# Four places in a PSUM bank for the output sum of a decode block, folded into two fresh banks near the end

## The chip, the cores and the metric

The kernel runs on one core of a Trainium2 chip. The metric is the device time of one execution in microseconds (us). Before the change, three runs gave 210.86, 211.17 and 211.27 us, median 211.17.

## What is computed

One decode step for 4 sequences of one token, model width 576. The normalised input feeds an attention block and an MLP block, and their outputs are added to the input:

```
xn = layernorm(A_x)
out = A_x + A(xn) + B(xn)

A: q = xn @ wq                      # 32 query heads of 128, 16 key/value heads
   k, v = the last 2048 of 8192 positions of k_cache, v_cache
   o = softmax(q k^T / sqrt(128)) v
   return o.reshape(4, 1, 4096) @ wo

B: (one position: its four shifts of h read only padding, so hs is 0)
   return xn + gelu(layernorm(xn) @ w3) @ w4     # w3: 576x4608, w4: 4608x576
```

All operands are bfloat16. The two products that end in the output, with `wo` (4096 rows) and with `w4` (4608 rows), and the sum xn + A_x are added up in PSUM, the matmul's accumulation memory, in one output sum of 4 x 576.

## The kernel before

The keys and values (16 heads, in 8 pairs, 4 MB each for K and for V) are read by indirect DMAs from the POOL queue (`load_kv`, L125) into three buffers. `flush_loads` issues the next load of a list written out by hand whenever a buffer comes free. The last items of the list are `wo`'s fourth quarter (L147) and `w4` (`load_w4`, L163). w4 has 36 rows of 128 x 576 (a "row" here is one 128-deep slice of its 4608 rows). It is loaded in six pieces, rows 0-17, 18-24, 25-29, 30-33, 34 and 35, each with a semaphore of its own, so a matmul waits only for its piece.

The schedule is manual: each engine carries out its instructions in the order of the program text. Each round t of the main loop transposes a pair's keys on DVE (L281), computes scores on PE (L395), and finishes the softmax, the product with V (L459) and the output projection of earlier pairs. Since two pairs' heads (four heads, or eight with the repeat) make one quarter of `wo`, every second round ends in `o_turn` (transpose), `o_sum`, `o_spread` (8 matmuls into R, L489), `o_pick` (two DVE operations on R, L499 and L502, that leave the operand `op`) and `o_proj` (L241).

The output sum is a PSUM tile of 128 partitions x 288 columns, cleared to 0 by L222. Its first 288 output columns stand in partitions 0 to 3, the other 288 in partitions 32 to 35. `acc_matmuls` (L238 to L242) adds a list of terms to it: each term is one 4-column weight and one 576-column row, split into two matmuls of 288 columns, one for each half. A matmul whose output starts at partition 0, 32, 64 or 96 uses the part of the PE array that belongs to that place. `o_proj` gives 8 terms, 16 matmuls; the w4 rows (`mlp_out`) give 36 terms, 72 matmuls.

In the last round (pair 7), `acc_split` (L229 to L235) moves the second half into a bank of its own: ACT copies 4 x 288 to SBUF (L232), and a float32 matmul with the identity writes it into a buffer of the pool of score tiles (tag S, three buffers; L234). A float32 matmul is carried out as two passes. After that, the two halves can be read by two engines at once. The end of the program is, from line 681: `o_scale`, `o_turn`, `o_sum`, `o_spread`, `o_pick`, `o_proj` for the last quarter, then w4's rows in order, then DVE copies the first half to `fin` (L694) and ACT the second (L696), and SP stores it (L697).

Of the kernel before, what the change touches and what calls it, by code (L numbers as in the profile page):

```python
# [8 lines left out]
ACT = mybir.ActivationFunctionType  # L9
ALU = mybir.AluOpType  # L10
AX = mybir.AxisListType
BF16 = mybir.dt.bfloat16
F32 = mybir.dt.float32
# [9 lines left out]
def kernel(  # L23
# [14 lines left out]
    nc = tc.nc  # L38
    P = 128
    B, Sq, D = A_x.shape  # L40
# [8 lines left out]
    NF = F // P  # L49
# [3 lines left out]
    QD = 32  # L53
# [6 lines left out]
    NI = 2  # L60
    CW = D // NI
    NW = SC * QD
# [20 lines left out]
    const = ctx.enter_context(tc.tile_pool(name="const", bufs=1))  # L83
    small = ctx.enter_context(tc.tile_pool(name="small", bufs=2))
    ps_s = ctx.enter_context(tc.tile_pool(name="ps_s", bufs=3, space=PSUM))
# [43 lines left out]
    first = wop.tile([P, WOR * D], BF16, tag="wo", name="first")  # L129
# [26 lines left out]
    W4_PIECES = [0, NFH, NF - 11, NF - 6, NF - 2, NF - 1, NF]  # L156
# [42 lines left out]
    ident_f = ident_w[:, 0:P]  # L199
# [18 lines left out]
    gT = const.tile([P, NF, B], BF16, name="gT")  # L218
    op = const.tile([P, WOR, B], BF16, name="op")

    acc = ps_acc.tile([P, CW], F32, name="acc")
    nc.vector.memset(acc[:], 0.0)  # L222

    accs = [acc, acc]

    def acc_of(i):
        return accs[i][i * QD:i * QD + B, 0:CW]

    def acc_split():  # L229
        rows = slice(QD, QD + B)  # L230
        half = const.tile([P, CW], F32, name="half")
        nc.scalar.activation(out=half[rows], in_=acc_of(1), func=ACT.Copy)  # L232
        accs[1] = ps_s.tile([P, NW], F32, tag="S", name="acc1")
        nc.tensor.matmul(out=acc_of(1), lhsT=ident_f[rows, rows], rhs=half[rows],  # L234
                         start=True, stop=False, skip_group_check=True)  # L235


    def acc_matmuls(terms):  # L238
        for lhsT, rhs in terms:
            for i in range(NI):  # L240
                nc.tensor.matmul(out=acc_of(i), lhsT=lhsT, rhs=rhs[:, i * CW:(i + 1) * CW],  # L241
                                 start=False, stop=False, skip_group_check=True)  # L242

    def layernorm(dst_f, dst_bf, src):
        st = small.tile([B, 2, nc.vector.BN_STATS_DIM], F32, tag="ln_st")
        nc.vector.bn_stats(out=st[:, 0, :], in_=src[:, 0:D // 2])
        nc.vector.bn_stats(out=st[:, 1, :], in_=src[:, D // 2:D])
        mv = small.tile([B, nc.vector.BN_AGGR_DIM], F32, tag="ln_mv")
        nc.vector.bn_aggr(out=mv[:], in_=st[:].rearrange("p a s -> p (a s)"))
        rstd = small.tile([B, 1], F32, tag="ln_rstd")  # L250
        nc.vector.tensor_scalar_add(out=rstd[:], in0=mv[:, 1:2], scalar1=eps)
        nc.gpsimd.tensor_tensor(out=rstd[:], in0=rstd[:], in1=neg_half[:], op=ALU.pow)  # L252
        nc.vector.tensor_scalar(out=dst_bf[:], in0=src[:], scalar1=mv[:, 0:1], scalar2=rstd[:, 0:1],
                                op0=ALU.subtract, op1=ALU.mult)
        if dst_f is not None:
            nc.vector.tensor_scalar(out=dst_f[:], in0=src[:], scalar1=mv[:, 0:1], scalar2=rstd[:, 0:1],
                                    op0=ALU.subtract, op1=ALU.mult)
# [20 lines left out]
    def k_transpose(t, q):  # L278
        src = kv_tiles["K", t][:].bitcast(I32)[:, q * QC:(q + 1) * QC, :].rearrange("p c (ib i) -> p ib c i", i=QD)
        kt = ktp.tile([P, 2, QC, QD], I32, tag="kt")  # L280
        nc.vector.transpose(out=kt[:], in_=src)  # L281
        kts[t, q] = kt
# [3 lines left out]
    for kb in range(NQD):  # L286
        nc.gpsimd.tensor_copy(out=sel[:, :, :, kb, :],
                              in_=ident_bf[:].rearrange("p (ib i e) -> p ib e i", ib=2, e=2))
# [23 lines left out]
    for g in range(2):  # L312
        nc.gpsimd.tensor_copy(out=same_j[:, g * 2 * QD:(g + 1) * 2 * QD].rearrange("p (e s j) -> p e s j", e=2, j=NJ),
                              in_=sel_j[:].unsqueeze(2).to_broadcast([P, 2, NSL, NJ]))
# [10 lines left out]
    xsum = xn_f  # L325
    nc.gpsimd.tensor_tensor(out=xsum[:], in0=xn_f[:], in1=x_bf[:], op=ALU.add)
    acc_matmuls([(ident_f[0:B, 0:B], xsum)])
    ln2_bf = part(D, B)
    layernorm(None, ln2_bf, xn_bf)
# [26 lines left out]
    for r in range(2):  # L356
        nc.vector.tensor_copy(out=q_bf[:, r],
                              in_=qT_ps[:, r].rearrange("p u (g x) -> p g u x", g=NQD)[:, :, :, 0:B])
    qs_ps = ps_m.tile([P, Hkv, 4, rep, B], F32, tag="m", name="qs_ps")
    for ie in range(4):  # L360
        ib, e = divmod(ie, 2)
        nc.tensor.matmul(out=qs_ps[:, :, ie], lhsT=sel[:, ib, e].rearrange("p k i -> p (k i)"),
                         rhs=q_bf.rearrange("p r g u b -> p (r g u b)"), start=True, stop=True)
    for kb in range(NQD):
        rows = slice(kb * QD, (kb + 1) * QD)
        dst = qz[rows, ZP:].rearrange("p (t i m) -> p t i m", i=4, m=P)[:, :, :, kb * QD:kb * QD + NJ]
# [20 lines left out]
    def k_scores(t, q, sl):  # L387
        u, s = q // 2, q % 2 * 2 + sl
        kt = kts[t, q][:].bitcast(BF16)
        if sl:  # L390
            kts.pop((t, q))
        for ie in range(4):
            ib, e = divmod(ie, 2)
            z0 = (t * 4 + ie) * P + ZP - s * NJ
            nc.tensor.matmul(out=S_ps[t, u][:], lhsT=qz[:, z0:z0 + P],  # L395
                             rhs=kt[:, ib, sl * SC:(sl + 1) * SC, e:2 * QD:2].rearrange("p c k -> p (c k)"),
                             start=False, stop=False, skip_group_check=True)
# [75 lines left out]
    def o_sum(t):  # L473
        oT = st.pop(("oT", t))
        v = oT[:].rearrange("p s (g x) -> p (s g) x", g=2).rearrange("p g (e x) -> p e x g", e=2)[:, :, 0:NJ]
        k = 2 * t % WOQ
        if k == 0:
            st["on"] = small.tile([P, WOH, B], BF16, tag="on", name="on")
        with nc.allow_low_precision("summed in float32"):
            nc.vector.reduce_sum(out=st["on"][:, k * rep:(k + 2) * rep, :].rearrange("p (e r) b -> p e (r b)", e=2),  # L480
                                 in_=v, axis=AX.X)

    def o_spread(h):
        if h % WOQ < WOQ - 1:
            return
        on = st.pop("on")
        R = ps_m.tile([P, WOR, WOH, B], F32, tag="m", name="R")
        for i in range(WOR):
            nc.tensor.matmul(out=R[:, i].rearrange("p h b -> p (h b)"),  # L489
                             lhsT=sel_wo[:, i].rearrange("p h d -> p (h d)"),  # L490
                             rhs=on[:].rearrange("p h b -> p (h b)"), start=True, stop=True)
        st["R"] = R

    def o_pick(h):
        if h % WOQ < WOQ - 1:
            return
        R = st.pop("R")
        mk = small.tile([P, WOR, WOH, B], BF16, tag="mk")
        nc.vector.tensor_tensor(out=mk[:], in0=R[:],  # L499
                                in1=own[:].unsqueeze(1).unsqueeze(3).to_broadcast([P, WOR, WOH, B]), op=ALU.mult)  # L500
        with nc.allow_low_precision("one term is not zero"):
            nc.vector.reduce_sum(out=op[:], in_=mk[:].rearrange("p i h b -> p i b h"), axis=AX.X)  # L502

    def o_proj(h):
        if h % WOQ < WOQ - 1:
            return
        acc_matmuls([(op[:, i, :], wo_tiles[h // WOQ][:, i, :]) for i in range(WOR)])
# [41 lines left out]
        nc.gpsimd.tensor_scalar(out=u[:], in0=u[:], scalar1=0.5, scalar2=0.5, op0=ALU.mult, op1=ALU.add)  # L549
        nc.gpsimd.tensor_tensor(out=gT[:], in0=u[:], in1=xs[:], op=ALU.mult)  # L550

    def mlp_out(lo, hi):
        w4 = w_tiles["w4"]
        acc_matmuls([(gT[:, u, :], w4[:, u, :]) for u in range(lo, hi)])


    G_AT = 3
# [84 lines left out]
    k_scores(hl, 1, 0)  # L642
    o_turn(o)
    k_scores(hl, 1, 1)
    acc_split()
    k_transpose(hl, 3)
    free_one()
    o_sum(o)
# [33 lines left out]
    o_turn(hl)  # L682
    o_sum(hl)
    o_spread(2 * hl + 1)
    o_pick(2 * hl + 1)
    o_proj(2 * hl + 1)
    for lo, hi in zip(W4_PIECES, W4_PIECES[1:]):
        mlp_out(lo, hi)

    fin = const.tile([B, D], out.dtype)  # L690
    for i in range(NI):
        dst = fin[:, i * CW:(i + 1) * CW]
        if i == 0:
            nc.vector.tensor_copy(out=dst, in_=acc_of(i))  # L694
        else:
            nc.scalar.activation(out=dst, in_=acc_of(i), func=ACT.Copy)  # L696
    nc.sync.dma_start(out=o2, in_=fin[:])  # L697


# [28 lines left out]
```

## Time and profile before

| what | us |
|---|---|
| median of three runs | 211.17 |
| the profiled execution | 210.84 |
| its span, first to last instruction | 209.07 |
| PE, DVE, ACT, POOL busy in the span | 145.9, 124.8, 29.7, 31.4 |
| start of the last `o_proj` | 200.63 |
| start of w4's first row on PE | 201.61 |
| start of the copies to fin | 206.36 |
| bytes moved | 87.32 MB, 418 GB/s over the span |

In the profile, PE stands for matmuls and PEld for the loads of their weights; DVE is VectorE, ACT ScalarE, POOL GpSimd, SP SyncE. A line of a timeline has the start in us from the span's start, the time to the end of the group, the engine, the line of the program, the operation, the tiles (written <- read), the shape and the number of instructions. In square brackets stands how long the engine was idle before it and what ended that. The page divides the span into 40 slices; one digit is a tenth of a slice, and PEclk is the clock that TensorE was granted, in tenths of the full one. The profiled execution's time holds 1.77 us that lie outside the span.

### The profile page before, as it was taken

How to read it: one execution, taken by the hardware profiler on the slowest of the kernel's cores; microseconds unless marked ns; L12 is line 12 of the kernel's file. 1: busy time of each engine (PE TensorE's matmuls, PEld its weight loads, DVE VectorE, ACT ScalarE, POOL GpSimd, SP SyncE). 2: the span in 40 equal slices, each digit the busy share in tenths (PEclk: the TensorE clock that was granted, in tenths of full speed). 3: DMA queues.
4: the chain of work that ended last, by engine and by line, in shares of the span. 5: the costliest groups of instructions: out<-in, count | busy, mean ns of one | idle time of the engine just before them, and what ended most of it. 6: DMA issues, size and time to landing. Idle time of an engine off the chain costs nothing.

```text
span 209.1 us, 2179 instructions
## 1 busy us (share of the span) xinstructions
PE 145.9 (70%) x879; PEld 60.6 (29%) x892; DVE 124.8 (60%) x177; ACT 29.7 (14%) x61; POOL 31.4 (15%) x62
## 2 busy tenths in 40 slices
PE   0249199649669943059998794587967937996974
PEld 0013033222215310014443431143324311453552
DVE  5410779994189700097928990989089818986120
ACT  6402500110102011003001201020002010303100
POOL 5680001003200110000133011001010161100000
PEclk9999859996957995558999999597999985998899
DMA  7999999999999999999999999999999999999991
GB/s 302 401 464 439 401 445 442 439 401 445 458 397 437 447 422 414 397 456 464 414 404 478 414 408 419 474 426 408 464 433 411 447 439 414 451 439 397 423 402 71
DMA packets 4156, 87.32 MB, mean 418 GB/s; under 512 B 489, under 2 KB 497, under 8 KB 1201
## 3 DMA queue, kind: packets, MB, share of 16 engines
q0 software_dynamic: 3840, 82.45, 91.8%
q1 hardware_dynamic: 296, 4.72, 5.5%
q8 instruction: 7, 0.11, 0.2%
q14 instruction: 5, 0.03, 0.0%
q10 hardware_dynamic: 8, 0.00, 0.0%
HBM read 87.17 MB, written 0.00 MB: 417 GB/s over the span
## 4 chain that ended last, share of the span: by engine, by line
DMA 42%; PE 32%; DVE 13%; issue 8%; POOL 3%; ACT 0%; POOLq 0%; DVEq 0%; ACTq 0%
DMA kn<-in_A_k_cache_dram,row 32%; PE S L395 14%; PE O L459 10%; DMA vn<-in_A_v_cache_dram,row 9%; DVE kt L281 8%; PE acc L241 3%; PE g_ps L522 1%; DVE pt L440 1%; PE oT L470 1%; PE gT_ps L535 1%; DVE mx L401 1%; POOL kn L125 0%; PE R L489 0%; PE S L383 0%; POOL rstd L252 0%
## 5 line engine op out<-in xcount | busy, mean ns | idle before, releaser
L281 DVE STREAM_TRANSPOSE kt<-kn 128x2048 int32<-128x2048 int32 x32 | 73.7, 2306 | 46.2 <-DMA kn<-in_A_k_cache_dram,row 44.0
L395 PE MATMUL S<-kt,qz 128*128 128x512 bf16 x243 | 76.2, 438 | 33.7 <-DVE kt L281 32.0
L395 PEld LDWEIGHTS <-qz 128*128 128x128 bf16 x256 | 23.4, 103 | 71.1 <-issue 54.4
L459 PE MATMUL O<-vn,pt 128*64 128x512 bf16 x256 | 36.0, 413 | 5.5 <-DVE kt L281 2.4
L440 DVE STREAM_TRANSPOSE pt<-E 64x512 bf16<-64x512 bf16 x32 | 22.1, 690 | 1.2 <-ACT E L431 0.9
L431 ACT ACTIVATE E<-S,bias 128x512 bf16<-128x512 f32 x16 | 10.9, 683 | 75.1 <-DVE bias L424 75.1
L125 POOL DMA_INDIRECT vn<-in_A_v_cache_dram,row x8 | 7.7, 962 | 91.3 <-DVE kt L281 87.2
L459 PEld LDWEIGHTS <-pt 128*64 128x64 bf16 x256 | 13.7, 116 | 22.2 <-issue 13.7
L464 ACT ACTIVATE O_sb<-O,rd 128x512 f32<-128x512 f32 x8 | 5.5, 687 | 62.5 <-PE O L459 62.5
L125 POOL DMA_INDIRECT kn<-in_A_k_cache_dram,row x8 | 7.9, 990 | 42.5 <-PE O L459 23.3
L401 DVE TENSOR_REDUCE mx<-S 128x1 f32<-128x512 f32 x16 | 10.7, 667 | 0.1
L522 PE MATMUL g_ps<-w_sb,ln2T 128*32 128x512 bf16 (+1 forms) x50 | 5.2, 489 | 2.9 <-DMA w_sb<-in_B_w_dram 2.9
L383 PE MATMUL S<-negbig,ohT 4*128 4x512 bf16 x16 | 6.4, 398 | 0.2 <-ACT E L431 0.2
L241 PE MATMUL acc<-wo_sb,op 128*4 128x288 bf16 x64 | 4.6, 286 | 1.0 <-DVE op L502 1.0
L480 DVE TENSOR_REDUCE on<-oT 128x16 bf16<-128x128 f32 x8 | 2.3, 286 | 4.9 <-PE oT L470 4.7
L470 PE MATMUL oT<-ident_w,O_sb 128*128 128x128 f32 x32 | 5.2, 286 | 0.0
L339 PE MATMUL q_ps<-wq_sb,xnT 128*32 128x512 bf16 x40 | 4.5, 629 | 0.9 <-DMA wq_sb<-in_A_wq_dram 0.9
L470 PEld LDWEIGHTS oT<-ident_w,O_sb 128*128 128x128 f32 x32 | 4.1, 149 | 2.2 <-issue 0.9
L241 PE MATMUL acc<-w_sb,gT 128*4 128x288 bf16 x72 | 4.7, 286 | 0.0
L163 POOL DMA_DIRECT2D w_sb<-in_B_w_dram x6 | 3.3, 579 | 8.1 <-DMA vn<-in_A_v_cache_dram,row 8.1
L424 DVE TENSOR_SCALAR bias<-bp 128x1 f32<-128x1 f32 x8 | 1.3, 159 | 5.3 <-PE bp L419 5.3
L404 DVE TENSOR_SCALAR dm<-sel_g,mx 128x8 bf16<-128x8 bf16 x16 | 3.9, 243 | 0.6
(100 smaller groups left out, 79.2 us busy)
## 6 DMA issues: line engine op xcount, KB each, us to landing
wo_sb<-in_A_wo_dram POOLq DMA_DIRECT2D x4, 1152.0 KB, 23.5
w_sb<-in_B_w_dram POOLq DMA_DIRECT2D x1, 4608.0 KB, 29.4
wq_sb<-in_A_wq_dram SPq DMA_DIRECT2D x1, 4096.0 KB, 13.8
w_sb<-in_B_w_dram POOLq DMA_DIRECT2D x1, 2592.0 KB, 29.1
w_sb<-in_B_w_dram POOLq DMA_DIRECT2D x2, 576.0 KB, 31.6
w_sb<-in_B_w_dram POOLq DMA_DIRECT2D x1, 1008.0 KB, 31.0
w_sb<-in_B_w_dram POOLq DMA_DIRECT2D x1, 720.0 KB, 32.2
wq_sb<-in_A_wq_dram SPq DMA_DIRECT2D x1, 512.0 KB, 3.3
```

What stands on the lines that cost most here:

```text
L125: nc.gpsimd.indirect_dma_start(tl[:].rearrange("p c d -> p (c d)"), None, k_rows if kind == "K" else v_rows, bass.IndirectOffsetOnAxis(ap= ...
L241: nc.tensor.matmul(out=acc_of(i), lhsT=lhsT, rhs=rhs[:, i * CW:(i + 1) * CW], start=False, stop=False, skip_group_check=True)
L281: nc.vector.transpose(out=kt[:], in_=src)
L383: nc.tensor.matmul(out=S_ps[t, u][:].rearrange("p (c k) -> p c k", k=QD), lhsT=ohT[:], rhs=negbig[:].unsqueeze(1).to_broadcast([B, SC, QD] ...
L395: nc.tensor.matmul(out=S_ps[t, u][:], lhsT=qz[:, z0:z0 + P], rhs=kt[:, ib, sl * SC:(sl + 1) * SC, e:2 * QD:2].rearrange("p c k -> p (c k)" ...
L401: nc.vector.reduce_max(out=mx[:], in_=S_ps[t, u][:], axis=AX.X)
L431: nc.scalar.activation(out=E[t, u][:].rearrange("p c k -> p (c k)"), in_=S_ps.pop((t, u))[:], func=ACT.Exp, scale=scale, bias=st["bias", t ...
L440: nc.vector.transpose(out=pts[t % 2 * NU + u][rows, :, e * QD:(e + 1) * QD], in_=e_in[rows])
L459: nc.tensor.matmul(out=O_ps[t][rows], lhsT=pts[t % 2 * NU + u][:, c, :], rhs=vn[:, u, :, c, :], start=(u == 0 and c < 2), stop=False, skip ...
L464: nc.scalar.activation(out=O_sb[t][:], in_=O_ps.pop(t)[:], func=ACT.Copy, scale=st.pop(("rd", t))[:, 0:1])
L470: nc.tensor.transpose(out=oT[:, s, :], in_=o[:, s, :], identity=ident_w[:, s * NJ:s * NJ + P])
L522: nc.tensor.matmul(out=g_ps[g * QD:(g + 1) * QD], lhsT=ln2T[:, k, :], rhs=cols[:, :, i0:i0 + n], start=(j == 0), stop=False, skip_group_ch ...
```

## The change

The output sum gets four places in its bank: partitions 0, 32, 64 and 96. Terms with an even number in their list go to the first two places, those with an odd number to the other two. `acc_split` is gone. Near the end, ACT copies the whole sum (128 x 288) to SBUF (`half`), two fresh banks are opened in the pool of score tiles (one for each half of the columns), and w4's rows from 25 on go there. Between rows 29 and 30, two float32 matmuls with a matrix of zeros and ones, `fold`, add `half`'s places 0 and 2 to the first bank, and 1 and 3 to the second. `fold` is made by one POOL operation in the preamble, behind the two identity matrices. w4's rows 0 to 17 are moved ahead of the last `o_pick` and `o_proj`. Loads and their order are not changed.

```diff
-    accs = [acc, acc]
-
-    def acc_of(i):
-        return accs[i][i * QD:i * QD + B, 0:CW]
-
-    def acc_split():
-        rows = slice(QD, QD + B)
+    def acc_of(g):
+        return acc[g * QD:g * QD + B, :]
+
+    def acc_matmuls(terms):
+        for k, (lhsT, rhs) in enumerate(terms):
+            for i in range(NI):
+                nc.tensor.matmul(out=acc_of(k % 2 * NI + i), lhsT=lhsT, rhs=rhs[:, i * CW:(i + 1) * CW],
+                                 start=False, stop=False, skip_group_check=True)
+
+    fold = const.tile([P, NI * B], F32, name="fold")
+    nc.gpsimd.tensor_tensor(out=fold[:].rearrange("p (i b) -> p i b", i=NI),
+                            in0=ident_f[:, 0:2 * QD].rearrange("p (i x) -> p i x", i=NI)[:, :, 0:B],
+                            in1=ident_f[:, 2 * QD:P].rearrange("p (i x) -> p i x", i=NI)[:, :, 0:B], op=ALU.add)
+    sums = []
+
+    def sum_of(i):
+        return sums[i][i * QD:i * QD + B, 0:CW]
+
+    def sum_open():
         half = const.tile([P, CW], F32, name="half")
-        nc.scalar.activation(out=half[rows], in_=acc_of(1), func=ACT.Copy)
-        accs[1] = ps_s.tile([P, NW], F32, tag="S", name="acc1")
-        nc.tensor.matmul(out=acc_of(1), lhsT=ident_f[rows, rows], rhs=half[rows],
-                         start=True, stop=False, skip_group_check=True)
-
-
-    def acc_matmuls(terms):
-        for lhsT, rhs in terms:
+        nc.scalar.activation(out=half[:], in_=acc[:], func=ACT.Copy)
+        for i in range(NI):
+            sums.append(ps_s.tile([P, NW], F32, tag="S", name=f"sum{i}"))
+        return half
+
+    def sum_matmuls(terms, first=False):
+        for k, (lhsT, rhs) in enumerate(terms):
             for i in range(NI):
-                nc.tensor.matmul(out=acc_of(i), lhsT=lhsT, rhs=rhs[:, i * CW:(i + 1) * CW],
-                                 start=False, stop=False, skip_group_check=True)
+                nc.tensor.matmul(out=sum_of(i), lhsT=lhsT, rhs=rhs[:, i * CW:(i + 1) * CW],
+                                 start=first and k == 0, stop=False, skip_group_check=True)
+
+    def sum_fold(half):
+        for i in range(NI):
+            nc.tensor.matmul(out=sum_of(i), lhsT=fold[:, i * B:(i + 1) * B], rhs=half[:],
+                             start=False, stop=False, skip_group_check=True)
...
-    def mlp_out(lo, hi):
+    def mlp_terms(lo, hi):
         w4 = w_tiles["w4"]
-        acc_matmuls([(gT[:, u, :], w4[:, u, :]) for u in range(lo, hi)])
+        return [(gT[:, u, :], w4[:, u, :]) for u in range(lo, hi)]
...
     k_scores(hl, 1, 1)
-    acc_split()
     k_transpose(hl, 3)
...
     o_spread(2 * hl + 1)
+    acc_matmuls(mlp_terms(*W4_PIECES[0:2]))
     o_pick(2 * hl + 1)
     o_proj(2 * hl + 1)
-    for lo, hi in zip(W4_PIECES, W4_PIECES[1:]):
-        mlp_out(lo, hi)
+    acc_matmuls(mlp_terms(*W4_PIECES[1:3]))
+    half = sum_open()
+    sum_matmuls(mlp_terms(*W4_PIECES[2:4]), first=True)
+    sum_fold(half)
+    sum_matmuls(mlp_terms(W4_PIECES[3], NF))
...
-            nc.vector.tensor_copy(out=dst, in_=acc_of(i))
+            nc.vector.tensor_copy(out=dst, in_=sum_of(i))
...
-            nc.scalar.activation(out=dst, in_=acc_of(i), func=ACT.Copy)
+            nc.scalar.activation(out=dst, in_=sum_of(i), func=ACT.Copy)
```

## The prediction

> **What bounds the kernel now.** I read the page's 40 slices first, for the DMA engines and the granted clock:
>
> ```profile
> PEclk9999859996957995558999999597999985998899
> DMA  7999999999999999999999999999999999999991
> ```
>
> The DMA engines are full in every slice but the first and the last, so the kernel is a stream of loads with the arithmetic beside it. The chain that ended last does not say so: its last part is PE, and only a small part of its tail is idle. The timeline of the last 9 us shows that part (start, length, engine, line):
>
> ```profile
> 199.31 0.35 PE L489 MATMUL R<-on,sel_wo 128*128 128x32 bf16 x8 [0.38 <-DVE on L480]
> 200.16 0.42 DVE L502 TENSOR_REDUCE op<-mk 128x32 bf16<-128x256 bf16 x1
> 200.63 1.15 PE L241 MATMUL acc<-wo_sb,op 128*4 128x288 bf16 x16 [0.97 <-DVE op L502]
> 201.61 4.72 PE L241 MATMUL acc<-w_sb,gT 128*4 128x288 bf16 x72
> 206.36 0.45 DVE L694 CAST fin<-acc 4x288 bf16<-4x288 f32 x1 [5.78 <-PE acc L241]
> ```
>
> It looks as if PE's 88 matmuls set the end. So I asked when w4's six pieces land: the POOL queue's timeline for the issue, and the DMA issues of the same short stretch for the time to landing (last column).
>
> ```profile
> 170.62 2.70 POOL L163 DMA_DIRECT2D w_sb<-in_B_w_dram  x5
> w_sb<-in_B_w_dram POOLq DMA_DIRECT2D x1, 2592.0 KB, 29.1
> w_sb<-in_B_w_dram POOLq DMA_DIRECT2D x1, 1008.0 KB, 31.0
> w_sb<-in_B_w_dram POOLq DMA_DIRECT2D x1, 720.0 KB, 32.2
> w_sb<-in_B_w_dram POOLq DMA_DIRECT2D x1, 576.0 KB, 33.1
> 181.41 0.55 POOL L163 DMA_DIRECT2D w_sb<-in_B_w_dram  x1 [8.09 <-DMA vn<-in_A_v_cache_dram,row]
> w_sb<-in_B_w_dram POOLq DMA_DIRECT2D x1, 144.0 KB, 24.6
> ```
>
> The first five issues start 0.52 to 0.55 us apart from 170.62 on. Landings: rows 0 to 17 at 199.7, 18 to 24 at 202.2, 25 to 29 at 203.9, 30 to 33 at 205.3, row 34 in between, row 35 at 181.41 + 24.6 = 206.0. Now the last eight matmuls alone, four rows:
>
> ```profile
> 205.57 0.76 PE L241 MATMUL acc<-w_sb,gT 128*4 128x288 bf16 x8
> ```
>
> A row is a pair of matmuls in two places, which run side by side. The 16 of o_proj take 1.15 us, 0.286 of it the length of the last one, so a row costs (1.15 - 0.286) / 7 = 0.123 us. Four rows should take 3 x 0.123 + 0.286 = 0.655 and took 0.76: the last row waited about 0.1 us, until 206.04. **The last transfer ends this execution, and PE reaches it with 0.1 us to spare.** What a faster PE can win behind it is nothing.
>
> The sum is made against the profiled execution: 210.84 us, of which 209.07 are span and 1.77 lie around it. The median of the runs is 211.17, 0.33 above.
>
> **The change, part by part.**
>
> (1) *fold*, on POOL: one more 128x8 operation between line 205 and the first power (L252), ahead of K's loads. The nearest rows are a 128x24 copy (0.23 us) and a memset (0.09). It lies in a stretch where POOL idles 1.42 us for DVE's rstd, so it costs 0; without the cover, 0.1 to 0.25 us on K's first issue, while wq's load keeps the DMA engines full anyway.
>
> (2) *acc_split goes*: one ACT copy (0.40 us) beside other work, and one float32 matmul of 0.57 us on the chain:
>
> ```profile
> 180.10 0.64 PE L234 MATMUL acc<-half,ident_w 4*4 4x288 f32 x2
> ```
>
> Next late is DVE's last transpose of K, which ends at 182.5, where PE came to its scores at about 182.7; I keep 0.2 us of the 0.57. op is ready at 200.4 in place of 200.63. The S buffer that acc1 took is not taken here any more; the sums take two when all earlier S tiles have been read.
>
> (3) *Rows 0 to 17 ahead of the last pick*: 36 matmuls go behind R, and o_proj's 16 are queued behind them. They wait for the 199.7 landing. With four places, two rows start per 0.123 us if four run side by side. The trace has that with 32-column weights:
>
> ```profile
> 15.03 4.46 PE L339 MATMUL q_ps<-wq_sb,xnT 128*32 128x512 bf16 x40 [0.94 <-DMA wq_sb<-in_A_wq_dram]
> ```
>
> Ten groups of four: (4.46 - 0.63) / 9 = 0.43 us a group at half clock, where 0.63 is the length of one. Four matmuls of line 395, 512 columns in one place, took 1.07 us at full clock, the last 0.39 of it: 0.23 each, so some 0.45 at half. Four places cost what one does. Bounds for four matmuls of 288: 0.123 (as here) and 0.246 (no better than two pairs); I take 0.123. Rows 0 to 17: 9 x 0.123 = 1.1 us, to 200.9; o_proj 4 x 0.123 = 0.5, to 201.4; then rows 18 to 24 wait for 202.2 and their last starts at 202.6, ends at 202.85. At the upper bound this ends at 203.8 to 204.1, which only just meets the 203.9 landing of rows 25 to 29.
>
> (4) *half, two fresh banks, fold*: ACT's copy of 128x288 (0.40, as L696) goes from 202.9 to 203.3. Rows 25 to 29 wait for 203.9 and take five pairs, 203.95 to 204.56. fold is two float32 matmuls of two passes. In L234 the second pass starts 0.24 after the first. In the early x sum (four passes in two places, 1.12 us at half clock) the places run side by side: 0.48 us. One after the other: 0.97. So fold ends at 205.05 (or 205.5). The copy is hidden behind the wait for 203.9, with 1.2 us to spare.
>
> (5) *Rows 30 to 35*: start at 205.33, the landing plus 0.045. Row 34 would start at 205.82, row 35 at 205.94, and must wait for 206.04, as before. If fold runs one after the other, row 35 starts at 206.14: 0.1 us late. The copies to fin and the store are the same.
>
> Sum on the path that sets the end: 0, bounds 0 and +0.1. So 210.85 against the profiled execution. Gain: PE's chain can now be over 2 us late at op (200.4 against 202.8) without anyone noticing, where before it had 0.1. So executions in which the clock makes the chain later lose less. The runs of before lie up to 0.43 above the profiled one; I expect those of after near the floor, **210.9**.
>
> **A rule against the change.** PE's tail now has pauses, and the clock follows PE's work in windows of 3.41 us. By windows on the grid of its changes (start and end, length, busy time of PE, PEld, DVE, ACT and POOL, then granted clock, DMA share, GB/s):
>
> ```profile
> 167.46:170.87 3.41, 1.70 (x11) 0.55 (x10) 0.00 (x0) 0.69 (x1) 1.74 (x3) 1.00 0.98 423
> 170.87:174.29 3.42, 0.37 (x1) 0.10 (x1) 2.73 (x2) 0.00 (x0) 2.46 (x5) 0.50 0.93 402
> 187.94:191.35 3.41, 1.54 (x19) 0.82 (x15) 1.57 (x3) 2.03 (x5) 0.00 (x0) 1.00 0.89 371
> 198.18:201.59 3.41, 2.06 (x32) 1.44 (x30) 1.14 (x3) 0.00 (x0) 0.00 (x0) 1.00 0.98 414
> 201.59:205.01 3.42, 3.42 (x60) 2.47 (x56) 0.00 (x0) 0.00 (x0) 0.00 (x0) 1.00 0.88 358
> ```
>
> Windows with 1.70 and 1.54 us of work were each followed by one at half clock, the one with 2.06 was not: the limit lies between 1.70 and 2.06. In the changed tail, 201.59 to 205.01 would hold 0.66 + 1.06 = 1.7 us. The Trainium skill ("TensorE: Matmul & The Clock Gate", "Why this matters for your kernels") asks only that no pause between bursts be over about 3 us. The tail's longest would be 1.1 us, so by the page the price is 0 and the sum stays 210.85. The window that ended at 191.35 had no pause over 1.5 us and lost the clock all the same, so the row is the stricter one.
>
> **Rivals.**
>
> *A, the half clock (slower).* If a window that ends between 203.8 and 205.0 is short of work, what follows runs at half clock: rows at 0.24, fold's passes at 0.48. Cut at 203.8: rows 25 to 29 to 205.15, fold to 206.1, row 35 starts at 207.3 and takes 0.43: +1.4 us. Cut at 204.9: row 35 at 206.5: +0.6. Typical +1.0: **211.9**. It decides where the window's end falls; 1.2 of 3.41 us of places do it, if the limit is where the two rows put it. For it: 1.7 us of work is on the limit. Against it: two thirds of the places miss it, and a cut at 205.0 costs only 0.6.
>
> *B, PE sets the end in the usual run (faster).* The profiled execution is the fastest of the four known. If in the others the last piece lands earlier, say by 0.35 us where row 34's does, and PE was late, then the change wins 0.35 below the profiled time: **210.5**. For it: only 0.1 us parts the two bounds, and 0.33 us lies between profile and median. Against: transfers are full throughout, and nothing shows them ending earlier.
>
> *C, the four places do not run side by side.* Then (3)'s upper bound holds, and the time is that of the forecast, 210.9 to 211.0.
>
> **How the numbers follow.** Forecast with C 0.54, A 0.24, B 0.22. About 0.2% (0.42 us) is what a measurement of this kernel can tell from no change: faster is under 210.75, slower over 211.59. A's cheap end stays inside (0.05), B's weak end too (0.02); the forecast gives 0.08 to faster and 0.01 to slower. Faster 0.20 + 0.08 = 0.28, slower 0.19 + 0.01 = 0.20, same 0.52. The range reaches to B's 210.4 and to 212.0 in A.
>
> **What would show it.** Right: the last w4 matmuls start within 0.1 us of the last landing at about 206.0, PE idle ahead of rows 18, 25 and 35, and groups of four in the time of one. Wrong: a clock of 0.5 ahead of 206 (A), last landings before 205.8 with an earlier end (B), or an end that moved with the landing of w4 itself, which nothing in this sum allows.

## The result, and the profile after

The changed kernel takes 210.86 us in the median of 22 runs (210.69 to 211.11). The kernel before, run beside it, takes 211.20 (210.73 to 212.04, 22 runs). The ratio is 0.9982, with a 95% interval of 0.9973 to 0.9990: a small gain, clear of zero and inside the 0.2% that the prediction called "same". The forecast was 210.9, in the range 210.4 to 212.0.

The two lists of runs say more than the medians. Their lowest values are the same (210.69 and 210.73). What differs is the upper end: before, 14 of the 22 runs lie above 211.11, the highest of after. The change did not make the best execution faster. It took the late ones away.

The profiled execution of the changed kernel took 211.11 us (span 209.3), at the slow end of its runs. The timeline of its tail, PE with the two other engines on the path (start, length, engine, line, tiles; in brackets the idle time before and what ended it):

```profile
198.90 0.35 PE L505 MATMUL R<-on,sel_wo 128*128 128x32 bf16 x8 [0.38 <-DVE on L496]
199.75 0.42 DVE L518 TENSOR_REDUCE op<-mk 128x32 bf16<-128x256 bf16 x1
200.02 1.27 PE L230 MATMUL acc<-w_sb,gT 128*4 128x288 bf16 x36 [0.77 <-DMA w_sb<-in_B_w_dram]
201.12 0.67 PE L230 MATMUL acc<-wo_sb,op 128*4 128x288 bf16 x16
202.44 0.66 PE L230 MATMUL acc<-w_sb,gT 128*4 128x288 bf16 x14 [0.66 <-DMA w_sb<-in_B_w_dram]
203.14 0.41 ACT L244 ACTIVATE half<-acc 128x288 f32<-128x288 f32 x1 [5.65 <-PE acc L230]
204.19 0.78 PE L252 MATMUL sum<-w_sb,gT 128*4 128x288 bf16 x10 [1.09 <-DMA w_sb<-in_B_w_dram]
204.79 0.65 PE L257 MATMUL sum<-half,fold 128*4 128x288 f32 x4
205.58 1.01 PE L252 MATMUL sum<-w_sb,gT 128*4 128x288 bf16 x12
206.62 0.45 DVE L713 CAST fin<-sum 4x288 bf16<-4x288 f32 x1 [6.45 <-PE sum L252]
```

PE now waits for a DMA ahead of rows 0, 18 and 25, as the brackets say. In the kernel before, the timeline shows no such wait: PE came late to the first pieces and waited 0.1 us for row 35, which only the rows' spacing shows. The last piece's issue on POOL, and its time to landing (last column):

```profile
181.74 0.55 POOL L163 DMA_DIRECT2D w_sb<-in_B_w_dram  x1 [8.19 <-DMA vn<-in_A_v_cache_dram,row]
w_sb<-in_B_w_dram POOLq DMA_DIRECT2D x1, 144.0 KB, 24.5
```

181.74 + 24.5 = 206.2. The last group of twelve is six rows; at 0.122 us a row it would take 5 x 0.122 + 0.286 = 0.90, and took 1.01, because row 35 waited for this landing. The landing is 0.25 us later than in the profiled execution of before (206.0), and so is the end of the span (209.3 against 209.1). In both, the last row starts with the last landing.

The profiles of all runs, those below included, say the same. In nine of the fourteen (before, after, e1, e2, e4, e6, e8, e10, e12) the last row starts within 0.05 us of the last landing, and there the time is always the landing plus 4.84 to 4.94 us, with landings from 203.9 to 206.3. In the other five (e3, e5, e7, e9, e11) PE comes later than the landing, and the time is the landing plus 5.3 to 7.1 us.

### The profile page after: what moved, and what is told of

The parts are those of the page before. It is cut to its first block, busy times and chain, and to the rows that moved or that the text cites. A ratio compares the mean times of both kernels' runs of the same rounds, so it can differ in the third digit from the quotient of the medians.

```text
span 209.3 us, 2197 instructions
## 1 busy us (share of the span) xinstructions
PE 144.9 (69%) x894; PEld 58.4 (28%) x894; DVE 124.8 (60%) x177; ACT 29.7 (14%) x61; POOL 31.6 (15%) x63
## 4 chain that ended last, share of the span: by engine, by line
DMA 62%; PE 18%; DVE 14%; POOL 2%; issue 2%; ACT 0%; POOLq 0%; DVEq 0%
DMA kn<-in_A_k_cache_dram,row 46%; DMA w_sb<-in_B_w_dram 16%; PE S L411 11%; DVE kt L297 9%; PE O L475 6%; DVE pt L456 1%; POOL w_sb L163 1%; DVE mx L417 1%; PE sum L252 1%; POOL vn L125 0%; PE oT L486 0%; DVE on L496 0%; POOL rstd L268 0%; POOL wo_sb L147 0%; DVE row L116 0%
## 5 line engine op out<-in xcount | busy, mean ns | idle before, releaser
L411 PE MATMUL S<-kt,qz 128*128 128x512 bf16 x256 | 78.4, 439 | 33.4 <-DVE kt L297 33.4
```

The source lines that it names most:

```text
L411: nc.tensor.matmul(out=S_ps[t, u][:], lhsT=qz[:, z0:z0 + P], rhs=kt[:, ib, sl * SC:(sl + 1) * SC, e:2 * QD:2].rearrange("p c k -> p (c k)" ...
```

## The experiments

Two theories were set against each other. **F**: the end is the later of two things, the last landing (near 206.0) and PE's chain; the landing is the same in both kernels, and the change only gives PE's chain room, so it helps the executions in which that chain comes late. **P**: PE's 88 last matmuls set the end, and four places gain because they make PE's work shorter. The prediction's rival A, the half clock behind pauses, was tried as well. All times are medians of runs, beside runs of the kernel before on the same chip; ratios are to those. The kernel before had a median of 211.02 to 211.20 in the several sets, so where times of different sets are compared, a difference of 0.2 us says nothing.

### The same PE work added to both kernels: e3, e4

```diff
+    fill = ps_m.tile([P, NW], F32, tag="m", name="fill")
     pv(hl, 0, 0, SC)
     pv(hl, 1, 0, SC)
+    for _ in range(6):
+        nc.tensor.matmul(out=fill[:], lhsT=ident_bf[:], rhs=sel_wo[...][:, 0:NW], start=True, stop=True)
     o_turn(a)
```

On the kernel before:

> The kernel before with six idle matmuls (128x512 into a tile that nobody reads, 0.227 us each, 1.36 us) on PE behind the last product with V, so that PE's chain is 1.36 us later. Theory F: PE had 0.1 us to spare in the profiled execution and less in the median one, so the end moves by 1.26 or more: 212.3 to 212.6. If PE had cover to hide it: 211.2.

Measured 212.30 us (7 runs, 211.86 to 214.90), ratio 1.0058 (1.0039 to 1.0077). The profiled execution is the one of 214.90; in it the loads ran late from the start and the last piece landed at 208.3 (182.78 + 25.5), and PE's last row still started 1.8 us behind that.

On the changed kernel:

> The changed kernel with the same six matmuls, 1.36 us. Theory F: o_proj ends at about 202.2, still ahead of the landing of rows 18 to 24 at 202.4, so nothing is lost: 210.9, at most 211.1. Rival P (PE's work sets the end here too): 212.2.

Measured 210.84 us (11 runs), ratio 0.9995 (0.9980 to 1.0010). So 1.36 us of PE work cost the kernel before 1.28 us (212.30 against 211.02 beside it) and the changed kernel nothing in the median. P falls here for the changed kernel. The tail of e4's profile:

```profile
197.16 1.47 PE L695 MATMUL fill<-sel_wo,ident_bf 128*128 128x512 bf16 x6
202.00 0.66 PE L230 MATMUL acc<-wo_sb,op 128*4 128x288 bf16 x16
202.49 0.66 PE L230 MATMUL acc<-w_sb,gT 128*4 128x288 bf16 x14
203.81 0.78 PE L252 MATMUL sum<-w_sb,gT 128*4 128x288 bf16 x10 [0.66 <-DMA w_sb<-in_B_w_dram]
```

The wait ahead of rows 18 to 24 is gone, used up by the added work; the one ahead of row 25 is still there, 0.66 us. The expectation's upper end was too low: 3 of the 11 runs are at 211.3 to 211.6. This kernel's room is smaller by the 1.36 us, and a chain that comes a further 1 us late (as in e1's profile below) may use up the rest; these three executions have no profile, so that is not shown.

### Less to load: e5, e6

The edit as e5 has it; e6 has the same index in `mlp_terms`.

```diff
         for lo, hi in zip(W4_PIECES, W4_PIECES[1:]):
             e, at = divmod(lo, NFH)
+            hi -= 6 if lo == 0 else 0
...
-        acc_matmuls([(gT[:, u, :], w4[:, u, :]) for u in range(lo, hi)])
+        acc_matmuls([(gT[:, u, :], w4[:, u - 6 if 12 <= u < 18 else u, :]) for u in range(lo, hi)])
```

On the kernel before:

> The kernel before without the load of w4's rows 12 to 17 (six rows, 0.88 MB, at 418 GB/s 2.1 us of transfer); the matmuls of these rows read rows 6 to 11 again, so PE's work is the same and the output's MLP part is not the reference's. All later landings come 2.1 us sooner. Theory F: PE is 0.1 us behind the landing in the profiled execution, so PE now sets the end: 0 to 0.15 us less, 211.0 to 211.2. If the landing set the end with room to spare: 209.1.

Measured 210.88 us (12 runs, 209.94 to 211.65), ratio 0.9983 (0.9966 to 1.0001), a little below the expected 211.0 to 211.2.

On the changed kernel:

> The changed kernel with the same six rows not loaded and the same rows read twice. Theory F: PE is 2 us ahead, so the end follows the landing: row 35 lands at 204.1, o_proj ends at 200.8 and rows 18 to 24 run at once: 208.8, 2.1 us less. Rival P (PE's work sets the end): 210.8.

Measured 208.90 us (4 runs, 208.75 to 209.11), ratio 0.9898 (0.9884 to 0.9912). With the landing some 2.1 us earlier, the changed kernel follows it by 2.0 us (from 210.86), and the kernel before by 0.25 (211.13 beside it to 210.88). The tail of e5, PE and the first copy, then the last piece's issue and landing:

```profile
201.95 4.58 PE L242 MATMUL acc<-w_sb,gT 128*4 128x288 bf16 x72
206.56 0.45 DVE L695 CAST fin<-acc 4x288 bf16<-4x288 f32 x1 [5.64 <-PE acc L242]
...
181.40 0.55 POOL L164 DMA_DIRECT2D w_sb<-in_B_w_dram  x1 [8.18 <-DMA vn<-in_A_v_cache_dram,row]
w_sb<-in_B_w_dram POOLq DMA_DIRECT2D x1, 144.0 KB, 22.5
```

The last piece is there at 203.9, and PE's 72 matmuls run on without a wait to 206.5. In e6 the last piece lands at 204.0 (181.43 + 22.6), and the last six rows take 1.03 us, 0.13 more than their spacing gives, because row 35 waits for it:

```profile
203.35 1.03 PE L253 MATMUL sum<-w_sb,gT 128*4 128x288 bf16 x12
```

So e5 shows PE's chain alone: its executions end anywhere from 209.9 to 211.7, a spread of 1.7 us. Put a floor of 210.7 to 211.1 under that list and it covers the range of the kernel before, though fewer runs lie high: 3 of 12 above 211.11, against 9 of 17 beside it.

### Why PE's chain differs between executions: e8, e10

```diff
     k_transpose(hl, 1)
     k_mask(hl, 0)
+    fill = ps_m.tile([P, NW], F32, tag="m", name="fill")
+    for _ in range(14):
+        nc.tensor.matmul(out=fill[:], lhsT=ident_bf[:], rhs=sel_wo[...][:, 0:NW], start=True, stop=True)
...
-    o_spread(2 * o + 1)
+    o_spread(2 * o + 1, 10)
```

The 10 in the last line stands for ten idle matmuls of 128x256 into R, ahead of R's own. The first pause is the one ahead of pair 7's keys (4.8 us in the profile of before), the second that of the softmax ahead of line 444 (1.5 us). On the kernel before, and nothing else:

> The kernel before with idle matmuls in two pauses of PE (14 of 128x512 while pair 7's keys land, 10 of 128x256 ahead of R while the softmax runs), so that no window of 3.41 us falls short of work; tail, places and order as before. Theory F with the clock as the cause of the late executions: PE's chain is earlier by 1.5 us or more in every execution, so the end is the landing: median 210.85, highest 211.15, as the changed kernel has, with none of the change. If late executions come from something else (transfers, start): 211.1, highest 211.9, as before.

Measured 210.86 us (11 runs, 210.69 to 211.07), ratio 0.9990 (0.9981 to 0.9999): the changed kernel's median and spread, with none of its parts. And with the smaller load of e5:

> The kernel before with w4's rows 12 to 17 not loaded (rows 6 to 11 read twice, so the MLP part is not the reference's) and the idle matmuls in the two pauses. There PE sets the end (209.9 to 211.7 without the idle matmuls). If the half clock behind the two pauses is what makes PE's chain late and different from one execution to the next: PE is 1.5 to 2.5 us earlier and the landing sets the end, 208.9 to 209.3. If not: 210.9.

Measured 208.90 us (4 runs, 208.81 to 209.00), ratio 0.9895 (0.9881 to 0.9910); e5 had 210.88. So idle matmuls in two pauses bring the end of all executions 2 us forward, onto the landing; what is left of the differences in PE's chain is hidden behind it. In the profiles, R of the last pair starts at 199.31 (before), 198.90 (after), 200.42 (e1), 199.65 (e5) with two stretches of half clock of 6.8 or 3.4 us and 3.4 us behind the pauses, and at 197.04 (e8) and 197.14 (e10) with none. The product with V behind the second pause shows the price. In the profile of before, 32 matmuls of line 459 took 5.29 us from 191.38; in e8, 3.64 (before, then e8):

```profile
191.38 5.29 PE L459 MATMUL O<-vn,pt 128*64 128x512 bf16 x32 [0.41 <-DVE pt L440]
190.76 3.64 PE L459 MATMUL O<-vn,pt 128*64 128x512 bf16 x32 [0.51 <-DMA vn<-in_A_v_cache_dram,row]
```

The half clock comes and goes on a grid of 3.41 us that lies differently in the profiles: the change of clock next to this pause is at 191.35 in before, 193.76 in e1 and 192.10 in e5. The runs of e5 go with that: the three fastest (209.94 to 210.23) had a mean granted clock of 0.885 to 0.902, the other nine (210.41 to 211.65) 0.869 to 0.878. That the half clock behind the two pauses makes the executions late is shown by e8 and e10; that the place of the grid alone sets one apart from the next is argued, since no late execution of the kernel before has a profile.

### The parts alone: e1, e2, e11

e1 moves w4's rows 0 to 17 ahead of the last pick in the kernel before; e2 keeps all of the change but that:

```diff
 e1, on the kernel before                     e2, on the changed kernel
     o_spread(2 * hl + 1)                         o_spread(2 * hl + 1)
+    mlp_out(*W4_PIECES[0:2])                -    acc_matmuls(mlp_terms(*W4_PIECES[0:2]))
     o_pick(2 * hl + 1)                           o_pick(2 * hl + 1)
     o_proj(2 * hl + 1)                           o_proj(2 * hl + 1)
-    for lo, hi in zip(W4_PIECES, ...):      +    acc_matmuls(mlp_terms(*W4_PIECES[0:2]))
+    for lo, hi in zip(W4_PIECES[1:], ...):       acc_matmuls(mlp_terms(*W4_PIECES[1:3]))
```

> The kernel before, with w4's rows 0 to 17 ahead of the last pick and nothing else: two places, the split into a second bank as before. Theory F (the last landing, near 206.0 us, sets the end; the median fell only because executions with a late PE chain are caught): rows 0 to 17 run from 199.8 to 202.0, o_proj to 203.0, the other 18 rows to 205.2, so PE has 0.8 us to spare in place of 0.1. Median 210.9, lowest 210.7, highest under 211.5. Rival P (the gain comes from PE's shorter work in four places): two places are not shorter, so 211.2, as before.

Measured 210.80 us (11 runs, 210.71 to 211.10), ratio 0.9991 (0.9981 to 1.0001). The spread is that of the changed kernel; the ratio's interval just touches 1. e1's profile happens to show a late chain, R at 200.42, 1.1 us later than in the profile of before, and the end was no later (span 209.0). It is a tie: the last 18 rows took 2.37 us, which is their spacing without a wait (17 x 0.122 + 0.286 = 2.36), and row 35 started 0.05 us behind its landing.

> The changed kernel with w4's rows 0 to 17 put back behind the last o_proj: four places, fold and fresh banks stay. Theory F: op at 200.2, o_proj to 200.7, rows 0 to 17 to 201.8, ahead of the 202.4 landing of rows 18 to 24, so the end is that of the changed kernel: median 210.9, highest 211.2. Rival P: the full gain as well, 210.9; a loss of the pick's 1 us of cover would give 211.2 or more if PE's order were what counts.

Measured 210.97 us (12 runs, 210.72 to 212.09), ratio 1.0003 (0.9985 to 1.0020). Three of the 12 runs lie at 212.0 to 212.1, against an expected highest of 211.2: F alone missed here. Four places without the move are no gain that can be told from zero. The three have no profile; e9 below shows one way in which such executions can come about.

e11 asks how far the move alone would go if less were loaded, as in e5:

> The kernel before with rows 0 to 17 ahead of the last pick, two places, and w4's rows 12 to 17 not loaded (rows 6 to 11 read twice, so the MLP part is not the reference's). The changed kernel has 208.9 at this lower floor and the kernel before 210.9. The move hides the pick's 1 us behind rows 0 to 17 and no more: PE ends at 205.2 in the profiled execution's grid, 1.2 us behind the lower floor: 209.9. If the move alone were as good as the whole change: 208.9.

Measured 210.00 us (5 runs), ratio 0.9944 (0.9931 to 0.9957), between e5 (210.88) and e6 (208.90). So where PE sets the end, the move gives about 0.9 us and the rest of the change (four places, no `acc_split`), with the move, at least another 1.1; at least, because e6 ends at its landing. At the full load most of both is hidden behind the landing.

### Pauses and the clock: e7, e9, e12

e7 leaves out 32 matmuls:

```diff
-    acc_matmuls(mlp_terms(*W4_PIECES[0:2]))
+    acc_matmuls(mlp_terms(0, 2))
```

> The changed kernel with the matmuls of w4's rows 2 to 17 left out (32 of 36), so the output's MLP part is not the reference's; all loads stay. PE's work ahead of the end falls by 1 us. Theory F alone: no change, 210.9. Rival A of the prediction (the clock follows PE's work in windows of 3.41 us): the window that ends near 201.7 holds 1.5 us of work or less in place of 2.26, the clock is halved there, and rows 25 to 35 and the fold run at half speed: 211.5 to 212.4, so less work would be slower.

Measured 212.20 us (6 runs, 211.55 to 212.49), ratio 1.0049 (1.0033 to 1.0064). **Less work, 1.3 us slower** than the changed kernel's 210.86. The windows of its profile (length, busy time of PE, PEld, DVE, ACT, POOL, then granted clock, DMA share, GB/s):

```profile
198.34:201.75 3.41, 1.34 (x29) 0.79 (x28) 1.14 (x3) 0.00 (x0) 0.00 (x0) 1.00 0.96 405
201.75:205.16 3.41, 2.41 (x26) 1.26 (x27) 0.00 (x0) 0.41 (x1) 0.00 (x0) 0.50 0.80 330
205.16:208.57 3.41, 2.48 (x18) 0.82 (x13) 0.45 (x1) 0.40 (x1) 0.00 (x0) 0.50 0.02 7
```

and the rows behind the landing, at twice the time per row:

```profile
205.03 1.17 PE L257 MATMUL sum<-half,fold 128*4 128x288 f32 x4
205.99 1.65 PE L252 MATMUL sum<-w_sb,gT 128*4 128x288 bf16 x12
```

A window with 1.34 us of PE work, with no pause over 1.4 us, is followed by half clock; the fold then takes 1.17 us where it took 0.65, and ends after the landing of rows 30 to 33 (205.2). That is rival A's mechanism, with a price, though the clock was cut at 201.75 and not between 203.8 and 205.0.

e9 is e2 with the idle matmuls of e8 in the two earlier pauses:

> The kernel with four places but rows 0 to 17 behind o_proj, with the same idle matmuls in the two pauses. It had three executions of twelve at 212.0. If those come from PE's chain arriving late because of the two earlier pauses: highest 211.2, median 210.85. If they come from the clock being cut in the tail itself (the pick's pause of 1 us and the waits for w4): they stay, one in four at 211.5 to 212.1.

Measured 211.61 us (12 runs, 210.84 to 212.38), ratio 1.0021 (1.0004 to 1.0038). Worse than either end of the expectation, since 7 of the 12 runs lie above 211.4: an earlier PE chain made it slower. Beside it, the same windows of e8, which has the same early chain and the two-place tail. First e9, then e8:

```profile
198.67:202.08 3.41, 1.27 (x36) 0.86 (x36) 0.00 (x0) 0.00 (x0) 0.00 (x0) 1.00 0.96 401
202.08:205.49 3.41, 2.78 (x28) 1.28 (x29) 0.00 (x0) 0.41 (x1) 0.00 (x0) 0.50 0.75 299
```

```profile
198.33:201.74 3.41, 3.29 (x52) 2.30 (x53) 0.00 (x0) 0.00 (x0) 0.00 (x0) 1.00 0.97 407
201.74:205.15 3.41, 2.03 (x28) 1.08 (x25) 0.00 (x0) 0.00 (x0) 0.00 (x0) 1.00 0.83 334
```

In e8, the slow rows fill the window while the transfers run (3.29 us), and the clock stays. In e9, the fast rows leave it empty (1.27 us), and the rows behind the landing run at half clock. The profiled executions took 211.23 (e9) and 210.78 (e8). In the profile of e9 the clock was back at 205.49; the executions of e9 at 212 have no profile.

e12 puts the same idle matmuls into the changed kernel:

> The changed kernel with the idle matmuls in the two earlier pauses, so that its PE chain is about 2 us earlier: R at 197.0, then PE waits for the 199.6 landing of rows 0 to 17. Theory F alone (the landing sets the end, an earlier PE chain can only help): 210.85, highest 211.1. Theory F with the clock rule of rival A (a window of 3.41 us with less than about 1.6 us of work halves the clock behind it): the pause of 2.6 us ahead of rows 0 to 17 and those ahead of rows 18 and 25 cut the clock in the tail, so an earlier chain makes it slower: median 211.5 to 212.2, lowest 210.8.

Measured 211.10 us (12 runs, 210.83 to 212.23), ratio 0.9999 (0.9983 to 1.0015). Right in direction, too strong in size: 3 of 12 runs are above 211.5, the median is only 0.24 above the changed kernel's. The profile shows why a cut need not cost anything:

```profile
196.59:200.00 3.41, 0.38 (x12) 0.35 (x15) 1.14 (x3) 0.00 (x0) 0.00 (x0) 1.00 0.89 380
200.00:203.42 3.42, 3.42 (x60) 2.03 (x63) 0.00 (x0) 0.00 (x0) 0.00 (x0) 0.50 1.01 421
```

The clock was halved at 200.0, but rows 0 to 24 and o_proj ended ahead of the landing of row 25 all the same, and behind that window, which their work at half clock had filled (3.42 us), the clock was back at 203.42, before the rows that matter.

## Why the prediction was right

- **The floor.** It read the last landing at 206.0 as the end, with PE 0.1 us ahead of it, and gave the sum on the path as 0. The lowest runs of both kernels are 0.04 us apart, and e5 and e6 show each side of the tie: take transfers away and, in the median, only the changed kernel follows.
- **The gain.** It said that the change is worth the room it gives PE's chain, that executions of before lie above the floor because of the clock, and that those of after should lie near it. The runs, e8 and e10 bear out both halves. The room was put at over 2 us; in e4, 1.36 of it was spent and 0.66 was left ahead of row 25. Rival B's observation (PE sets the end in the usual run) holds, going by the times, for more than half the runs of before, but what it made of it, an end below the profiled floor, does not.
- **(1) fold on POOL.** Nothing of it is seen in the time; it was not tried by itself.
- **(2) acc_split.** The last scores now wait 0.18 us for DVE's last transpose, as foreseen. The step left out a term: the third quarter's o_proj (L230) also runs in four places, 0.66 us in place of 1.15. R came at 198.90 rather than 199.31, although pair 7's keys landed 0.3 us later in that execution.
- **(3) Four places.** Rows 0 to 17 took 1.27 us: 8 groups x 0.122 + 0.286. A group of four, 0.122 us, costs what a pair did before; rival C is out. The row of line 339, from which the prediction took this, was put at half clock by its lengths (0.63 us against 0.39); the page's PEclk row has 9 there, but the trace's first clock record is at 20.7.
- **(4) half and fold.** 0.41 for the copy and 0.24 between the passes, both places side by side: the lower of the two bounds.
- **(5) The last rows.** Row 35 waited, as before.
- **Rival A.** The mechanism is real: e7, cut earlier than the prediction had it, lost 1.34 us, inside the 0.6 to 1.4 worked out. It did not decide the changed kernel: none of 22 runs lies above 211.11. The sharp limit between 1.70 and 2.06 was wrong: the window 201.67 to 205.08 of the changed kernel held 1.66 us of work and kept the clock, below the 1.70 that lost it in before:

```profile
201.67:205.08 3.41, 1.66 (x32) 0.94 (x28) 0.00 (x0) 0.41 (x1) 0.00 (x0) 1.00 0.92 374
```

There is luck in this. By the prediction's own share (1.2 of 3.41 us of places), 7 or 8 of the 22 runs should have had a window ending in the bad stretch, with some 1.7 us of work, and windows with that much work were cut in some profiles (last section). Why none of the 22 shows it is open.

## What to carry to other kernels

Where a stream of loads and a chain of compute end within a fraction of a microsecond of each other, look at the landing of the last bytes before counting the instructions that end the chain: the work saved in front of it shows only in the executions in which compute was late. Take the spread of many runs as a measurement; equal lowest times and a shorter upper end mean room, not speed. And work that is made shorter ahead of a fixed wait can cost the clock behind it, so ask what PE will do with the time it saves.

## What the runs showed of the hardware that was not expected

The clock's limit is not sharp in PE's busy time. Counted over the windows at full clock in the 14 profiles (570 of them), those with under 1.53 us of busy PE in 3.41 were all followed by half clock and those with over 2.02 by none; between them lie both.

The 16 parts of a transfer do not land together. In the profile after, the 16 parts of the first load of keys landed within 0.35 us of each other, those of w4's last piece within 1.73 (204.53 to 206.26): in the course of the kernel more and more of the parts land 0.5 to 1.7 us behind the first. The page's queue `q8 instruction` moves 16 KB packets that take 0.88 to 0.96 us each, seven in this execution:

```profile
q8 instruction: 7, 0.11, 0.2%
```

Whether these are what sets the parts apart was not tried. If so, the floor itself could come down, since the last row waits for the latest part.
